# Sixteen rows of a weight load, taken out of the late transfer and fetched early by GpSimd as single packets

## The chip, the cores and the metric

One core of one Trainium2 chip. The metric is the device time of the slowest (here the only) core in microseconds (us), as the median of the timed executions. MB in the profile are 10^6 bytes; a row of 16 KB is 16,384 bytes, a K load of 4096 KB is 4.19 MB.

## The reference

One decoding step: grouped attention over a long cache, a small dense block, and a residual sum. Nearly all the work is reading the two caches from HBM (2 x 134 MB).

```python
# x: (1, 1, 512); k_cache, v_cache: (1, 8, 65536, 128) bf16; 32 query heads, 4 for each K/V head
xn = layernorm(x)
q = xn @ wq                                        # wq: 512 x 4096
p = softmax(q @ k.T * 128 ** -0.5)                 # per head, over 65536 keys
o = p @ v
a = o.reshape(4096) @ wo                           # wo: 4096 x 512, 4.2 MB
b = gelu(xn @ w1 + b1) @ w2 + b2                   # w1: 512 x 1792, w2: 1792 x 512
out = x + a + b
```

## The kernel before

K and V come in sixteen pairs, each of two K loads of 4 MB (slots 0 and 1 of the buffer `kv`) and 8 MB of V (the upper half of `kv`). All big loads are issued by the SP engine into one queue, each as soon as PE has freed its slot. When the last K slots are free, `wo` is loaded into them: three pieces of 2, 1 and 0.5 MB for the first 28 heads, then two pieces for the last four heads.

```python
kv = sb("kv", [128, NSLOT * TPD * DH], BF)          # 4 slots of 32 KB for each partition
...
WP = ...                                            # (0, 4), (4, 2), (6, 1): groups of heads
wo_sb = kv[:, 0:GE * HPG * D].rearrange("p (r n) -> p r n", n=D)
wl_sb = kv[:, wl_at:wl_at + HPG * D].rearrange("p (h n) -> p h n", h=HPG)

def dma_wo():
    for i, (g0, n) in enumerate(WP):
        r = n * HPG
        sch.dma(SP, lambda g0=g0, n=n, r=r: sp.dma_start(
            out=wo_sb[:, g0 * HPG:g0 * HPG + r, :],
            in_=A_wo[g0 * HPG * DH:(g0 + n) * HPG * DH, :].rearrange("(p r) n -> p r n", r=r)),
            wsem[i], writes=[f"wo{i}"] + (["slot0"] if i == 0 else []))
    ...                                             # two wl pieces, into slot 1

for i in range(NU // 2):                            # 16 pairs
    ...
    body(i)                                         # transposes of K, scores, softmax, P @ V
...
for i, (g0, n) in enumerate(WP):                    # the product with wo, at the very end
    for r in range(g0 * HPG, (g0 + n) * HPG):
        for kt in range(KT):
            fin_mm(kt, oX_bf[:, r:r + 1], wo_sb[:, r, kt * 128:(kt + 1) * 128], ["oX", f"wo{i}"], ...)
```

The first piece is the one that the change touches: 128 partitions, 16 KB for each, so 128 rows of 16 KB.

## Time and profile before

| | before |
|---|---|
| time, median of 4 | 658.37 us (658.2 to 658.52) |
| span of the profiled run | 656.5 us |
| bytes moved by the main DMA queue | 280.50 MB |
| PE busy | 82% of the span |
| last landing of a load | 653.7 us |

The page of the kernel before: busy tenths of the DMA engines and GB/s in 40 slices, then the DMA queues (packets, MB, and the time that their packets took, as a share of sixteen engines' span).

```profile
DMA  8999999999999999999999999999999999999997
GB/s 369 438 436 426 429 430 433 439 425 461 401 441 439 421 453 413 437 427 445 433 417 449 417 445 421 427 457 411 447 419 447 429 419 441 423 459 408 431 433 295
...
q1 hardware_dynamic: 8616, 280.50, 99.2%
```

Between the first and the last slice the sixteen DMA engines are busy for 90% or more of every slice. The kernel ends when 280.5 MB have gone through them.

The windows table of the kernel before: for each stretch (us), its length and the busy time of each engine, the granted clock, the DMA share and GB/s.

```profile
240.00:282.00 42.00, 35.85 (x839) 34.23 (x837) 19.97 (x41) 17.32 (x31) 0.09 (x1) 0.80 1.00 432
300.00:600.00 300.00, 254.02 (x6048) 244.33 (x6045) 129.06 (x258) 119.05 (x216) 0.62 (x7) 0.77 1.00 433
634.00:654.00 20.00, 18.06 (x565) 16.43 (x562) 8.09 (x27) 5.14 (x16) 0.09 (x1) 0.68 0.90 376
```

The last but one column is the DMA share: 1.00 in the middle. So I expected time that an engine loses here to move the end (in e2 below it did: 16.6 us lost by the last pair, 16.9 in the time).

The chain that ended last in the kernel before, in order of time (start, length, what): one pair in the middle, and the end.

```profile
237.20 28.38 DMA kv<-in_A_k_cache_dram
265.63 7.16 PE pst L590 x96
275.40 28.96 DMA kv<-in_A_k_cache_dram
...
635.45 1.53 PE pst L590 x24
636.99 16.42 DMA kv<-in_A_wo_dram
```

Of each 38.8 us of a pair the chain spends 28 to 29 in a K load that is on its way, because it was queued behind others: at the 433 GB/s of the table its 4.19 MB alone need 9.7. The last thing that the kernel waits for is `wo`.

Two more facts come from the trace's records of single packets and of semaphore updates. First, the time of a packet follows its bytes: 614 ns for 16 KB, 1216 ns for 32 KB, 2422 ns for 64 KB, 27 GB/s for each engine. Second, every load has sixteen landing marks, as many as it has packets in flight at once (sixteen at 220, 300 and 640 us). I read them as one mark for each DMA engine. Read so, how far apart they lie shows how unequally the engines are loaded:

```
kernel before, landing marks in us     first     9th       last      last - first
a K load                              224.79    225.72    226.80     2.0
a K load one pair later               263.57    264.51    265.58     2.0
a V load                              331.43    332.35    333.42     2.0
last pair, first half of V            632.01    633.12    634.04     2.0
last pair, second half of V           641.73    642.84    643.75     2.0
first wo piece (2 MB)                 646.62    647.74    648.64     2.0
last wo piece                         651.88    652.88    653.73     1.9
```

A difference of 2 us that arose early (0.5 us at 21 us, 2.0 at 72 us) stays to the end, while the DMA share stays near 1.00.

### The profile page before, as it was taken

What the parts mean: (1) busy time and instruction counts of PE and PEld (TensorE: products, weight loads), DVE (VectorE), ACT (ScalarE), POOL (GpSimd) and SP (SyncE); (2) the same over time, 40 slices, a digit from 0 to 9 for tenths busy, and PEclk for the clock granted to TensorE, in tenths of its full rate; (3) what the DMA queues carried; (4) which work ended last, traced back from release to release, by engine and by line L of the source; (5) the groups of instructions that cost most, each with busy time, mean ns of one, the idle gap of its engine ahead of it and who ended that gap; (6) DMA issues with size and microseconds to landing.
All of it is one profiled execution on the core that took longest, in us unless ns stands there. A gap on an engine that the chain in (4) does not pass through costs nothing.

```text
span 656.5 us, 27968 instructions
## 1 busy us (share of the span) xinstructions
PE 539.3 (82%) x12682; PEld 512.1 (78%) x12682; DVE 275.7 (42%) x574; ACT 244.9 (37%) x454; POOL 2.9 (0%) x27
## 2 busy tenths in 40 slices
PE   2388699999789797878969787896978879797897
PEld 0187698988689697868969786896968779686896
DVE  3244162635435172442616245171634516254353
ACT  0134153534425152351605335161443516144251
POOL 0000000000000000000000000000000000000000
PEclk9788597878759596885959778596877859687595
DMA  8999999999999999999999999999999999999997
GB/s 369 438 436 426 429 430 433 439 425 461 401 441 439 421 453 413 437 427 445 433 417 449 417 445 421 427 457 411 447 419 447 429 419 441 423 459 408 431 433 295
DMA packets 8774, 280.65 MB, mean 427 GB/s; under 512 B 1082, under 2 KB 1596, under 8 KB 1724
## 3 DMA queue, kind: packets, MB, share of 16 engines
q1 hardware_dynamic: 8616, 280.50, 99.2%
q8 instruction: 8, 0.13, 0.1%
q10 hardware_dynamic: 148, 0.01, 0.0%
q14 instruction: 2, 0.02, 0.0%
HBM read 280.50 MB, written 0.00 MB: 427 GB/s over the span
## 4 chain that ended last, share of the span: by engine, by line
DMA 63%; PE 34%; issue 2%; DVE 0%; SPq 0%
DMA kv<-in_A_k_cache_dram 61%; PE pst L590 27%; PE pss L610 4%; DMA kv<-in_A_wo_dram 3%; PE pO L681 2%; PE pA L637 0%; PE pA L648 0%; DVE pmax L618 0%; PE pA L697 0%; PE pss L805 0%; DVE gmax L639 0%; DVE diag L641 0%; SPq L470 0%; SPq L467 0%; SPq L463 0%
## 5 line engine op out<-in xcount | busy, mean ns | idle before, releaser
L590 PE MATMUL pst<-ident_bf,kv 128*128 128x128 bf16 x4096 | 284.3, 236 | 34.0 <-DMA kv<-in_A_k_cache_dram 33.9
L600 ACT ACTIVATE kt_ring<-pst 128x1024 bf16<-128x1024 bf16 x192 | 195.6, 1027 | 312.1 <-PE pst L590 310.7
L590 PEld LDWEIGHTS pst<-ident_bf,kv 128*128 128x128 bf16 x4096 | 266.0, 107 | 42.4 <-DMA kv<-in_A_k_cache_dram 35.5
L598 DVE COPY kt_ring<-pst 128x1024 bf16<-128x1024 bf16 x320 | 210.7, 687 | 121.1 <-PE pst L590 118.7
L681 PE MATMUL pO<-P_bf,kv 128*128 128x4 bf16 x4096 | 115.1, 166 | 37.1 <-DMA kv<-in_A_v_cache_dram 32.1
L681 PEld LDWEIGHTS pO<-P_bf,kv 128*128 128x128 bf16 x4096 | 113.6, 104 | 38.5 <-DMA kv<-in_A_v_cache_dram 33.1
L610 PE MATMUL pss<-q_cur,kt_ring 128*128 128x4 bf16 x4096 | 111.9, 164 | 4.9 <-issue 4.9
L610 PEld LDWEIGHTS pss<-q_cur,kt_ring 128*128 128x128 bf16 x4096 | 109.3, 96 | 5.1 <-issue 5.1
L659 ACT ACTIVATE P_bf<-pss,negm 128x128 bf16<-128x128 f32 x128 | 50.9, 547 | 67.6 <-DVE negm L651 67.6
L690 DVE COPY o_all<-pO 128x4 f32 (+1 forms) x32 | 5.2, 161 | 120.3 <-PE pO L681 119.5
L618 DVE TENSOR_REDUCE pmax<-pss 128x4 f32<-128x512 f32 x32 | 22.1, 691 | 68.8 <-PE pss L610 68.8
L659 ACT ACTIVATION_READ_ACCUMULATOR P_bf<-pss,negm 128x1 f32 x128 | 35.3, 276 | 0.0
L648 PEld LDWEIGHTS pA<-diag,ones_f 4*128 4x128 f32 x64 | 12.6, 245 | 17.8 <-DVE diag L641 16.2
L637 PE MATMUL pA<-ident_f,pmax 128*4 128x128 f32 x64 | 14.0, 305 | 12.5 <-DVE pmax L618 12.5
L648 PE MATMUL pA<-diag,ones_f 4*128 4x4 f32 x64 | 15.4, 309 | 10.0 <-DVE diag L641 10.0
L637 PEld LDWEIGHTS pA<-ident_f,pmax 128*4 128x4 f32 x64 | 2.9, 84 | 15.7 <-DVE pmax L618 14.0
L639 DVE TENSOR_REDUCE gmax<-pA 4x1 f32<-4x128 f32 x32 | 8.8, 274 | 9.1 <-PE pA L637 9.1
L673 DVE COPY sums_all<-sums 128x8 f32 (+1 forms) x16 | 2.7, 171 | 23.4 <-ACT P_bf L659 23.4
L697 PE MATMUL pA<-sums_all,ones_f 128*128 128x128 f32 x32 | 12.4, 491 | 0.0
L651 DVE TENSOR_SCALAR negm<-pA 128x4 f32<-128x4 f32 x32 | 5.1, 161 | 10.8 <-PE pA L648 10.8
L697 PEld LDWEIGHTS pA<-sums_all,ones_f 128*128 128x128 f32 x32 | 8.1, 312 | 0.0
L641 DVE TENSOR_SCALAR diag<-ident_f,gmax 4x4 f32<-4x4 f32 x32 | 7.0, 218 | 1.1
(78 smaller groups left out, 49.5 us busy)
## 6 DMA issues: line engine op xcount, KB each, us to landing
kv<-in_A_k_cache_dram SPq DMA_DIRECT2D x32, 4096.0 KB, 27.5
kv<-in_A_v_cache_dram SPq DMA_DIRECT2D x4, 4096.0 KB, 23.2
kv<-in_A_wq_dram SPq DMA_DIRECT2D x1, 4096.0 KB, 12.2
kv<-in_B_w_dram SPq DMA_DIRECT2D x2, 1792.0 KB, 18.0
kv<-in_A_wo_dram SPq DMA_DIRECT2D x1, 2048.0 KB, 23.0
kv<-in_A_wo_dram SPq DMA_DIRECT2D x1, 1024.0 KB, 25.1
kv<-in_A_wo_dram SPq DMA_DIRECT2D x1, 512.0 KB, 25.9
kv<-in_A_wo_dram SPq DMA_DIRECT2D x1, 384.0 KB, 16.4
```

The source lines that it names most:

```text
L590: lambda tb=tb, at=at, b=b, tt=s * TPB + t: pe.transpose(pst[tb][:, at * 128:(at + 1) * 128], slot[b][:, tt, :], ident_bf[:, :]),
L598: e, fn = DVE, lambda tb=tb, dst=dst: dve.tensor_copy(out=dst, in_=pst[tb][:, :])
L600: e, fn = ACT, lambda tb=tb, dst=dst: act.activation(out=dst, in_=pst[tb][:, :], func=ACTF.Copy)
L610: lambda k=k, kb=kb, at=at, t=t: pe.matmul(pss[k][:, at:at + HPG], lhsT=kt_ring[:, kb * BCOL + t * 128:kb * BCOL + (t + 1) * 128], rhs=q_c ...
L618: lambda k=k: dve.tensor_reduce(out=pmax[:, :], in_=pss[k][:, 0:CW].rearrange("p (t j) -> p j t", j=HPG), axis=AX.X, op=ALU.max),
L637: sch.op(PE, lambda: pe.matmul(pA[0:HPG, PA_ST:PA_ST + 128], lhsT=pmax[:, 0:HPG], rhs=ident_f[:, :], start=True, stop=True), reads=["pmax" ...
L639: sch.op(DVE, lambda: dve.tensor_reduce(out=gmax4[:, :], in_=pA[0:HPG, PA_ST:PA_ST + 128], axis=AX.X, op=ALU.max), reads=["pA"], writes=[" ...
L641: sch.op(DVE, lambda: dve.tensor_scalar(out=diag4[:, :], in0=ident_f[0:HPG, 0:HPG], scalar1=gmax4[0:HPG, 0:1], scalar2=None, op0=ALU.mult) ...
L648: sch.op(PE, lambda: pe.matmul(pA[:, PA_SB:PA_SB + HPG], lhsT=ones_f[0:HPG, 0:128], rhs=diag4[0:HPG, 0:HPG], start=True, stop=True), reads ...
L659: lambda k=k, at=at, j=j, src=src: act.activation(out=P_v[k][:, :, j], in_=src[:, :, j], func=ACTF.Exp, bias=negm[:, at:at + 1], scale=1.0 ...
L681: lambda k=k, t=t: pe.matmul(pO[:, 0:HPG], lhsT=vslot[:, k * TPD + t, :], rhs=P_v[k][:, t, :], start=t == 0, stop=t == TPD - 1),
L697: sch.op(PE, lambda: pe.matmul(pA[:, PA_SUM:PA_SUM + NC], lhsT=ones_f[:, :], rhs=sums_all[:, :], start=True, stop=True), reads=["ones_f", ...
```

## The change

The first `wo` piece gets a buffer of its own, `wa`, so it need not wait for slot 0. Of its 128 rows only 112 stay in the late transfer. The other sixteen, partitions 112 to 127, are fetched early, before the fifth pair, by sixteen GpSimd transfers of 8179 elements, one row each. 8179 is a prime number, chosen so that a row is not cut into equal pieces. The 13 elements left of each row come by one small SP transfer. The idea is to have an eighth of the piece out of the way before the end.

```diff
+    NS = 16
+    WA = WP[0][1] * HPG
+    LP = WA * D - 13
+    wa = sb("wa", [128, WA * D], BF)
+    wo_sb = kv[:, WA * D:GE * HPG * D].rearrange("p (r n) -> p r n", n=D)
 ...
+    def dma_rest():
+        for p in range(128 - NS, 128):
+            sch.dma(POOL, lambda p=p: pool.dma_start(out=wa[p:p + 1, 0:LP], in_=src_wa()[p:p + 1, 0:LP]), sem_wa,
+                    writes=["wo0r"], total=16 * NS)
+        sch.dma(SP, lambda: sp.dma_start(out=wa[128 - NS:128, LP:WA * D],
+                                           in_=src_wa()[128 - NS:128, LP:WA * D]), sem_wb, writes=["wo0s"])
+
     def dma_wo():
         for i, (g0, n) in enumerate(WP):
             r = n * HPG
+            if i == 0:
+                sch.dma(SP, lambda: sp.dma_start(out=wa[0:128 - NS, :], in_=src_wa()[0:128 - NS, :]), wsem[i],
+                        writes=["wo0"])
+                continue
 ...
-                wsem[i], writes=[f"wo{i}"] + (["slot0"] if i == 0 else []))
+                wsem[i], writes=[f"wo{i}"] + (["slot0"] if i == 1 else []))
 ...
+        if i == 4:
+            dma_rest()
         body(i)
 ...                                    # and the final product reads wa for the first sixteen heads
```

More of the change, by code (lines that the diff above doesn't have):

```diff
@@ L340, in bass_parallel_sum__gqa_block_cached__dense_activation_gelu__decode_kernel, with wo_row @@
         g0 += n
-    wo_sb = kv[:, 0:GE * HPG * D].rearrange("p (r n) -> p r n", n=D)
+    NS = 16
[3 more added lines that the diff above has]
+    wo_sb = kv[:, WA * D:GE * HPG * D].rearrange("p (r n) -> p r n", n=D)
+    def wo_row(r, cols):
+        return wa[:, r * D + cols.start:r * D + cols.stop] if r < WA else wo_sb[:, r - WA, cols]
     wl_at = TPD * DH
@@ L389, in bass_parallel_sum__gqa_block_cached__dense_activation_gelu__decode_kernel @@
     lsem = [sch.dsem(f"lsem{i}") for i in range(2)]
+    sem_wa, sem_wb = sch.dsem("dwa"), sch.dsem("dwb")
     sem_vb = sch.dsem("dvb")
@@ L473, in bass_parallel_sum__gqa_block_cached__dense_activation_gelu__decode_kernel, with src_wa @@
     WH = (HPG - 1, 1)
+    def src_wa():
+        return A_wo[0:WA * DH, :].rearrange("(p r) n -> p (r n)", r=WA)
+    def dma_rest():
[4 more added lines that the diff above has]
+                                           in_=src_wa()[128 - NS:128, LP:WA * D]), sem_wb, writes=["wo0s"])
     def dma_wo():
@@ L477, in dma_wo @@
             r = n * HPG
+            if i == 0:
+                sch.dma(SP, lambda: sp.dma_start(out=wa[0:128 - NS, :], in_=src_wa()[0:128 - NS, :]), wsem[i],
+                        writes=["wo0"])
+                continue
             sch.dma(SP, lambda g0=g0, n=n, r=r: sp.dma_start(
-                out=wo_sb[:, g0 * HPG:g0 * HPG + r, :],
+                out=wo_sb[:, g0 * HPG - WA:g0 * HPG - WA + r, :],
                 in_=A_wo[g0 * HPG * DH:(g0 + n) * HPG * DH, :].rearrange("(p r) n -> p r n", r=r)),
-                wsem[i], writes=[f"wo{i}"] + (["slot0"] if i == 0 else []))
+                wsem[i], writes=[f"wo{i}"] + (["slot0"] if i == 1 else []))
         h0 = 0
@@ L812, in bass_parallel_sum__gqa_block_cached__dense_activation_gelu__decode_kernel @@
             for kt in range(KT):
-                fin_mm(kt, oX_bf[:, r:r + 1], wo_sb[:, r, kt * 128:(kt + 1) * 128], ["oX", f"wo{i}"], False, False,
+                fin_mm(kt, oX_bf[:, r:r + 1], wo_row(r, slice(kt * 128, (kt + 1) * 128)), ["oX", f"wo{i}"] + ["wo0r", "wo0s"] * (i == 0), False, False,
                        r == (g0 + n) * HPG - 1 and kt == KT - 1)
```

## The prediction

> **What bounds it now.** The DMA engines, nearly from end to end. The page's queue part has the main queue busy 99.2% of the span (280.5 MB, 427 GB/s); the windows table has a DMA share of 1.00 at 433 GB/s for 200 to 600 us. The trace's packets of 16, 32 and 64 KB take 614, 1216 and 2422 ns: time follows bytes, 27 GB/s per engine. The SP queue issues each K load 27.5 us (median) before it lands, of which 4 MB needs 9.7: large slack. PE is 82% busy but waits for K and V. The chain of waits ends in 16.4 us of "DMA kv<-wo"; the last landing is at 653.7, the span ends at 656.5.
>
> The sixteen landing marks of each transfer differ by 2.0 us from about 70 us to the end: five engines are 1.7 to 2 us behind the foremost, after instruction fetches (16 KB, 1.02 to 1.12 us each, 27 to 84 us). The span ends with the last of them.
>
> **What the change does.**
> - It removes no bytes. 112 rows of 16 KB stay in the last loads (7 per engine, not 8: 0.61 us less there); 16 rows move to about 217 us, when the fifth V has landed.
> - The first wo piece loses its wait for slot 0 (12.7 us on the SP queue). It ends at 625.6, when two V halves (8 MB, landing 634.0 and 643.7) are still queued, so no engine starved for it. Gain about 0.
> - The 13 elements left over: 16 descriptors of 26 bytes. The trace's 28-byte packets take 9 ns. Under 0.1 us.
> - GpSimd: 16 issues, in the 38.8 us between two V flags.
> - PE, DVE, ACT: the same order of instructions.
>
> **How the early rows share the engines.** [...]sixteen transfers give one row to each engine. No run here shows it yet. Then every engine carries as many bytes as before: +0.61 us early, -0.61 us late. Against it: all sixteen rows lie in partitions 112 to 127[...]. I expect a loss of 0 to 2 us.
>
> **Predicted:** 658.9 us, range 657.0 to 661.3. Faster by over 2%: 0.01; within 2%: 0.97; slower by over 2%: 0.02.
>
> **What would show it.** Right: a new GpSimd queue with 16 packets of 16 KB near 217 to 245 us; K and V landings after 260 us are 0.5 to 2 us later than before; the last wo landing still closes the chain; the first wo piece is issued near 613 but lands only after V, near 648. The spread of the landing marks stays 2 us or grows to 3.
>
> **What would make it wrong.** If [...]all 16 rows fall on one engine, it carries 15 more rows: 15 x 0.61 = 9 us later (667). If the engines that get or lose rows happen to be the laggards, the spread shrinks and up to 1.5 us is won. If an issue takes several us, a V flag is late. If packets of a second queue cost double, as the instruction fetches do, 0.5 us more is lost.

The forecast's sum: 658.4 us before, 0.61 us more for each engine early and 0.61 less late (a row of 16 KB took 614 ns), under 0.1 us for the leftover, and a loss of 0 to 2 us for the early rows; it came to 658.9 us. Three passages are cut. They argued why the rows would spread over the engines, and why rows on sixteen neighbouring partitions would cost something, which gave the 0 to 2 us. No trace or run of this case shows the rules that they rested on. So "one row to each engine" and the 0 to 2 us stand as assumptions. In the expectations of the experiments, the clauses that rested on such rules are cut too.

## The result, and the profile after

| | before | after |
|---|---|---|
| time, median of 4 | 658.37 us | 679.06 us (678.16 to 679.52) |
| span of the profiled run | 656.5 us | 677.6 us |
| MB of all packets | 280.65 | 280.65 |

The change is slower by 20.7 us, far above the predicted range (657.0 to 661.3). The ratio is 1.0313 (95% interval 1.0295 to 1.0331). Ratios here are the mean time of one kernel's fast runs over that of the other's of the same rounds, so they are not quite the ratio of the medians quoted.

The page of the kernel after: the same parts as shown of before.

```profile
DMA  9999999999999999997999999999999999999993
GB/s 371 433 459 403 430 433 449 433 418 449 418 449 418 438 412 402 436 408 308 433 431 429 433 433 427 431 422 433 433 414 453 414 445 416 449 427 420 431 304 119
...
q1 hardware_dynamic: 8632, 280.24, 97.5%
q0 software_dynamic: 512, 0.26, 0.2%
```

The bytes are the same. A new queue, q0, holds the GpSimd transfers: 512 packets for 16 transfers, of which 16 carry a row (16,358 bytes) and 496 are of 4 bytes. Slice 19 (from 305 us) falls to 308 GB/s with a busy digit of 7, and the last slice (from 661 us) to 119 with a 3: there some engines have nothing to do. The slice before the last (from 644 us) moves only 304 GB/s although its digit is 9: there the engines are busy, and their packets take longer (the 16 KB packets of the 112 rows 1088 ns on average instead of 614).

The windows table after:

```profile
240.00:282.00 42.00, 23.29 (x598) 22.11 (x596) 10.32 (x23) 9.18 (x23) 0.09 (x1) 0.67 0.98 408
300.00:600.00 300.00, 248.31 (x5963) 238.59 (x5960) 122.67 (x251) 113.76 (x211) 0.70 (x8) 0.76 0.99 424
650.00:675.00 25.00, 18.96 (x570) 16.52 (x567) 8.37 (x28) 5.43 (x18) 0.09 (x1) 0.65 0.64 179
```

Between 240 and 282 us PE works 23.3 us instead of 35.9: it waits. The chain after says for what:

```profile
239.09 40.99 DMA kv<-in_A_k_cache_dram
280.13 7.97 PE pst L613 x96
290.72 29.05 DMA kv<-in_A_k_cache_dram
...
651.74 1.53 PE pst L613 x24
653.28 20.87 DMA kv<-in_A_wo_dram
```

One K load is in the chain for 41.0 us instead of 28.4, and the wo load at the end for 20.9 instead of 16.4. These are two separate steps. GpSimd issued its sixteen transfers just before the first of them, in one go (the timeline of GpSimd after: start, length, what):

```profile
217.17 0.09 POOL L456 MEMSET flag<- 1x1 f32 x1 [38.73 <-DMA kv<-in_A_v_cache_dram]
217.72 8.30 POOL L489 DMA_DIRECT2D wa<-in_A_wo_dram  x16 [0.46 <-issue]
266.23 0.09 POOL L456 MEMSET flag<- 1x1 f32 x1 [40.21 <-DMA kv<-in_A_v_cache_dram]
```

An issue took 0.52 us, and the flag of the sixth V was late only because the V was. GpSimd itself is not in the way.

The landing marks answer most of the question:

```
kernel after, landing marks in us      first    15th     last     last of before   later by
a K load                              224.77   227.26   228.08    226.80            1.3
a K load one pair later               264.15   268.46   280.09    265.58           14.5
a V load                              339.09   339.62   348.84    333.42           15.4
a K load                              543.99   545.84   553.38    537.03           16.4
last pair, first half of V            641.16   643.06   650.37    634.04           16.3
last pair, second half of V           650.91   654.60   665.17    643.75           21.4
first wo piece (1.75 MB)              658.75   662.32   669.41    648.64           20.8
last wo piece                         665.49   667.19   674.47    653.73           20.7
```

From the second line on a single engine is late, 7 to 12 us behind the fifteenth. The loss comes in three terms. The early step is 15.4 us (up to the V load). A slow growth of 0.9 us follows, up to the last pair. The late step is 4.4 us (20.7 - 16.3), at the time when the 112 rows are loaded.

The packet records show the late step on the late engine itself, which can be followed there, since it alone still moves V after 653.7 us. It has V left to load when the other engines begin the 112 rows (their packets run from 650.4 to 661.4 us). Five of its V packets of 32 KB, from 651.25 us on, take 2373, 2328, 2262, 2352 and 1746 ns instead of 1216: 5.0 us too much. Its own seven rows come after that, when the others are done with the piece, and take 611 to 618 ns each. They are one fewer than before, which gives 0.6 us back.

The single packets show the early step at work. This is from the packet records of the kernel after; each line begins within 20 ns of where the one before ends:

```
start us   took ns   queue      bytes
226.179     1525     q1         32768
227.700      774     q0         16358    a row
228.461     1538     q1         32768
231.215      782     q0         16358    a row   (after one more packet of q1)
```

The sixteen rows follow each other like this, between 221.9 and 280.1 us, and never overlap. They take turns with packets of the main queue, one or two of these between two rows. A row takes 755 ns on average and the 32 KB packet after it about 320 ns more than its 1216. So a row costs this engine about 1.08 us, not the 0.61 of 16 KB in the main queue.

My theory then (A): all sixteen rows go through one engine, and the 112-row transfer is slow by itself. The rivals: (B) the rows are spread over the engines and hinder each other, since all are written to sixteen neighbouring partitions; (C) the second queue or GpSimd costs something in itself; and for the late step, that it only follows from the late engine.

### The profile page after: what moved, and what is told of

Read it like the earlier page. It is cut to its first block, busy times and chain, and to the rows that moved or that the text cites. A ratio compares the mean times of both kernels' runs of the same rounds, so it can differ in the third digit from the quotient of the medians.

```text
span 677.6 us, 27986 instructions
## 1 busy us (share of the span) xinstructions
PE 539.3 (80%) x12682; PEld 511.3 (75%) x12682; DVE 275.7 (41%) x574; ACT 245.2 (36%) x454; POOL 11.2 (2%) x43
## 2 busy tenths in 40 slices
DMA packets 9303, 280.65 MB, mean 414 GB/s; under 512 B 1611, under 2 KB 2125, under 8 KB 2253
## 4 chain that ended last, share of the span: by engine, by line
DMA 64%; PE 33%; issue 2%; DVE 0%; SPq 0%
DMA kv<-in_A_k_cache_dram 61%; PE pst L613 26%; PE pss L633 4%; DMA kv<-in_A_wo_dram 3%; PE pO L704 2%; PE pA L660 0%; PE pA L671 0%; DVE pmax L641 0%; PE pA L720 0%; PE pss L830 0%; DVE gmax L662 0%; DVE diag L664 0%; SPq L479 0%; SPq L476 0%; SPq L472 0%
## 5 line engine op out<-in xcount | busy, mean ns | idle before, releaser
L671 PE MATMUL pA<-diag,ones_f 4*128 4x4 f32 x64 | 15.4, 309 | 10.0 <-DVE diag L664 10.0
L456 POOL MEMSET flag<- 1x1 f32 x16 | 1.4, 88 | 652.8 <-DMA kv<-in_A_v_cache_dram 614.1
L489 POOL DMA_DIRECT2D wa<-in_A_wo_dram x16 | 8.3, 527 | 0.5 <-issue 0.5
## 6 DMA issues: line engine op xcount, KB each, us to landing
kv<-in_A_wo_dram SPq DMA_DIRECT2D x1, 384.0 KB, 20.9
```

Source lines behind the costliest of these rows:

```text
L489: sch.dma(POOL, lambda p=p: pool.dma_start(out=wa[p:p + 1, 0:LP], in_=src_wa()[p:p + 1, 0:LP]), sem_wa, writes=["wo0r"], total=16 * NS)
L671: sch.op(PE, lambda: pe.matmul(pA[:, PA_SB:PA_SB + HPG], lhsT=ones_f[0:HPG, 0:128], rhs=diag4[0:HPG, 0:HPG], start=True, stop=True), reads ...
```

## The experiments

Eleven kernels ran, all with correct results. Variants called "late load of all 128" fetch all 128 rows of the piece again at the end, after waiting for the early ones. The early rows are then redundant, and the early step stands alone. The common part of those is:

```diff
-                sch.dma(SP, lambda: sp.dma_start(out=wa[0:128 - NS, :], in_=src_wa()[0:128 - NS, :]), wsem[i],
-                        writes=["wo0"])
+                sch.dma(SP, lambda: sp.dma_start(out=wa[:, :], in_=src_wa()), wsem[i],
+                        writes=["wo0", "wo0r", "wo0s"])
```

| run | early rows | late load | time us | before, same chip | ratio |
|---|---|---|---|---|---|
| e1 | none | 128 rows | 658.40 | 658.39 | 1.0000 |
| e2 | 16 single GpSimd rows, 112-127 | 128 rows | 675.25 | 658.39 | 1.0260 |
| e3 | one SP transfer of rows 112-127 | 112 rows | 666.74 | 658.39 | 1.0122 |
| e4 | 16 GpSimd rows of 8192 elements | 128 rows | 662.45 | 658.39 | 1.0059 |
| e5 | 4 GpSimd transfers of 4 rows | 128 rows | 667.88 | 658.44 | 1.0139 |
| e6 | 8 single rows, 112-119 | 128 rows | 665.25 | 658.44 | 1.0106 |
| e7 | 8 single rows, 0-3 and 32-35 | 128 rows | 661.59 | 658.44 | 1.0049 |
| e8 | 16 single rows, issued by SP | 128 rows | 677.19 | 658.44 | 1.0288 |
| e9 | none | 64 + 64 rows | 664.94 | 658.49 | 1.0102 |
| e10 | 16 single rows, 0-15 | 128 rows | 672.57 | 658.49 | 1.0215 |
| e11 | first 1024 columns of all 128 rows | the other 7168 columns | 658.49 | 658.49 | 0.9999 |

### e1: the buffer alone

The late load of all 128, and no `dma_rest()`.

> The control: the new buffer alone, all 128 rows in one late SP transfer, nothing from GpSimd. Every theory that puts the loss into the sixteen early rows or into the 112-row load expects the time of before, 658.4 us within 0.5, and landing marks of the wo pieces as before (last at 653.7). If the time is above 660, the buffer or the earlier place in the queue costs something itself.

Measured: 658.40 us, ratio 1.0000 (0.9983 to 1.0016). The buffer and the missing wait for slot 0 neither cost nor win anything. The prediction was right in this.

### e2: the early rows alone

The late load of all 128, `dma_rest()` as in the change.

> The sixteen GpSimd rows as in the change, but the late load takes all 128 rows again (the sixteen are loaded twice, with the same bytes, the second time after waiting for the first). Theory A (one engine carries all sixteen rows, about 1.08 us each, and the 112-row load is a second, separate cost): 658.4 + 15.5 + 0.8 at the early step, no step of 5 us at the V1/wo stage, so 674 to 676 us, with one engine 9 us or more behind the others. Theory B (the rows are spread over the engines[...]): no single laggard. If the late step of 5 us is only a consequence of the laggard and not of 112 rows: 679 to 680 us.

Measured: 675.25 us, 16.9 above before. One engine is over 6 us behind the fifteenth to the end. The last pair's first half of V lands 16.6 us later than before and the last wo piece 16.6 us later: there is no late step. So the early rows cost 16.6 us by themselves, the slow growth included. The step of 4.4 us belongs to the 112-row load, and does not follow from the late engine, which is here too.

### e3: the sixteen rows in one transfer

```diff
-        for p in range(128 - NS, 128):
-            sch.dma(POOL, ...)
-        sch.dma(SP, ...)
+        sch.dma(SP, lambda: sp.dma_start(out=wa[128 - NS:128, :], in_=src_wa()[128 - NS:128, :]), sem_wb,
+                writes=["wo0r", "wo0s"])
```

> The sixteen rows by one SP transfer of 16 rows at the same place, the late load with 112 rows as in the change. Theory A: one row for each engine, so no laggard; the early step falls below 2 us and the late load of 112 rows still costs 3 to 5 us: 661 to 664 us. Theory B[...]: [...]the early step stays and the time is 674 us or more. If the 112-row load costs nothing without the laggard: 658.5 to 660 us.

Measured: 666.74 us, a miss for both theories. Theory A is right that the step of 15 us is gone: no single engine is far behind. But in the profiled run (668.62 us, the slowest of four) the early transfer still costs 4.6 us (the K load of 226.80 before lands at 231.44) instead of under 2, and the late step is 5.6 us. In the packet records the packets of the main queue beside the early transfer take half as long again to twice their time: of the sixteen packets in flight at 217.0 us, one for each engine, eight are of 32 KB with 1.9 to 2.5 us (usual: 1.2) and eight of 64 KB with 3.8 to 5.1 (usual: 2.4). The 16 KB packets of the late load take 1103 ns on average, against 614 before. This fits the hindrance that B named; how it comes about was not shown. It is not what made the change's early step of 15.4 us, but not a small thing either: sixteen rows of 16 KB, 0.6 us of bytes if each engine carries one, cost 4.6 us this way.

### e4: whole rows, a length that 16 divides

```diff
-    LP = WA * D - 13
+    LP = WA * D
```

The small SP transfer is left out with it; late load of all 128.

> GpSimd transfers of whole rows (8192 elements, divisible by 16) in place of 8179, no leftover; the late load takes all 128 rows again. Theory A1 (one engine because 8179 is prime[...]): now each row is cut into sixteen pieces, all engines share, 658.8 to 661 us, and the GpSimd queue has 256 packets of 1 KB. Theory A2 (one partition means one engine, whatever the length): 16 packets of 16 KB on one engine, 674 to 676 us.

Measured: 662.45 us. The q0 queue now has 256 packets of 1 KB in place of sixteen of 16 KB, so each row is cut into sixteen pieces, and the single late engine is gone (last and fifteenth mark are 0.2 us apart at the end). So it was the length, 8179 instead of 8192, that put each row on one engine. The time is 1.5 us above the range: the last engine loses 4.2 us where the range left room for 0.4 to 2.6. The reason was not shown.

### e5: does the first engine move on?

```diff
-        for p in range(128 - NS, 128):
-            sch.dma(POOL, lambda p=p: pool.dma_start(out=wa[p:p + 1, 0:LP], ...
+        for a, n in [(112, 4), (116, 4), (120, 4), (124, 4)]:
+            sch.dma(POOL, lambda a=a, n=n: pool.dma_start(out=wa[a:a + n, 0:LP], in_=src_wa()[a:a + n, 0:LP]), sem_wa,
+                    writes=["wo0r"], total=16 * 4)
```

> Four GpSimd transfers of four rows (4 x 8179 elements[...]) in place of sixteen of one row; late load of all 128 rows. If the first engine of each transfer moves on by the number of engines used[...], the sixteen rows fall on sixteen engines: no engine over 3 us behind after 300 us, 660 to 663 us. If every transfer starts at the same engine[...], four engines carry four rows each: they end 3 to 5 us behind the rest (4 x 1.08, less up to 2 us of lead): 662 to 665 us, and the landing marks after 300 us show a group of four late ones.

Measured: 667.88 us, outside both ranges. The landing marks alone don't decide, since all engines are late: the first mark of the V load of 333 us comes 5.5 us later than before, the last 9.7. The packet records decide. The nine packets below follow each other end to start within 10 ns each time, so they are read as one engine's, and four rows are among them:

```
start us   took ns   queue      start us   took ns   queue
221.92      1076     q0 row     230.29       949     q0 row
222.99      2684     q1         231.24      2168     q1
225.68      1213     q1         233.41      1215     q1
226.88       939     q0 row     234.62      1026     q0 row
227.83      2462     q1
```

So one engine carried one row of each of the four transfers: the first engine did not move on. The same records show how all engines lost. Of the sixteen packets in flight at 223.95 us, one is a row (1.88 us) and the other fifteen are 32 KB packets that take 2.0 to 3.5 us instead of 1.2; the same happens twice more (1.9 to 3.3 us at 228.2, 1.9 to 3.4 at 231.3). Each of these transfers writes four neighbouring partitions. Why the packets of the other engines take longer meanwhile was not shown.

### e6 and e7: eight rows, on two kinds of partitions

```diff
-        for p in range(128 - NS, 128):
+        for a, n in [(p, 1) for p in range(112, 120)]:                      # e6
+        for a, n in [(p, 1) for p in (0, 1, 2, 3, 32, 33, 34, 35)]:         # e7
```

> Half the single rows: eight GpSimd transfers, rows 112 to 119; late load of all 128. One engine at 1.08 us for each row, which led by about 2 us: 8 x 1.08 - 2 = 6.6 us behind, so 665 to 667 us. If the loss is a fixed cost of having such transfers and not of the rows, it stays near 675.

> Eight single rows again, but those of partitions 0 to 3 and 32 to 35[...]. [...]the packets take 0.61 and the time is 661 to 663 us (8 x 0.61 - 2 = 2.9). If the extra cost is that of the second queue, it is 665 to 667 us as with rows 112 to 119.[...]

The first range of e7 is for a cost that depends on which partitions a row is written to.

Measured: 665.25 us (6.8 above before) and 661.59 us (3.15 above). The rows take 756 ns in e6, and the packets after them 325 ns too long. In e7 a row takes 611 ns, and the packet after it is not longer at all (2 ns less on average). Both agree with the sums written before: 8 x 1.08 - 2.0 = 6.6 and 8 x 0.61 - 2.0 = 2.9, where 2.0 is the lead that this engine had. So the second queue costs nothing by itself here. The two runs differ only in the partitions that the rows are written to (756 ns on 112 to 119, 611 ns on 0 to 3 and 32 to 35). So the partitions make a row dear or cheap; by what mechanism was not shown.

### e8: the same single rows from SP

```diff
-            sch.dma(POOL, lambda p=p: pool.dma_start(...
+            sch.dma(SP, lambda p=p: sp.dma_start(...
```

> The sixteen single-row transfers of 8179 elements issued by SP in place of GpSimd, in the main queue; late load of all 128. They all go to one engine here too. Packets in the same queue without alternation: if each costs 0.61 us, 16 x 0.61 - 2 = 7.8 us, 666 to 668 us; if 0.75 to 0.8 us[...], 668 to 671 us; if 1.08 us as on GpSimd, 674 to 676 us.

Measured: 677.19 us, above all three ranges, though again one engine is far behind (over 14 us behind the fifteenth in the next K load). In the main queue the rows stand behind each other without packets between them, from 214.5 to 233.5 us, so one row takes 1.19 us, about twice 0.61. 16 x 1.19 - 2.0 = 17 us. The K load of 226.80 before lands at 244.00, 17.2 us later; the rest of the loss of 18.8 comes afterwards and was not tested. That GpSimd issued the rows is not the reason.

### e9: the late load in two halves

```diff
-                sch.dma(SP, lambda: sp.dma_start(out=wa[0:128 - NS, :], in_=src_wa()[0:128 - NS, :]), wsem[i],
-                        writes=["wo0"])
+                for h in range(2):
+                    sch.dma(SP, lambda h=h: sp.dma_start(out=wa[64 * h:64 * h + 64, :], in_=src_wa()[64 * h:64 * h + 64, :]),
+                            wsem[i], writes=["wo0"], total=32)
```

No `dma_rest()`.

> Nothing early, nothing from GpSimd; the late load of 128 rows cut into two SP transfers of 64 rows (partitions 0 to 63, then 64 to 127). Each engine still moves eight rows of 16 KB. [...]its 16 KB packets take about 1.2 us instead of 0.61 and the late load takes up to 4.9 us longer: 661 to 664 us. If the 112-row load is slow for another reason (its odd shares of seven rows)[...], the time is that of before, 658.4 within 0.6.

The first range is for a transfer to fewer than 128 partitions that is slow for that alone.

Measured: 664.94 us, 6.45 above before, 0.9 above the range. The last landing marks agree with before within 0.25 us from 200 us up to the last pair's first half of V (634.21 against 634.04); after that, the second wo piece is 6.7 us later. The 16 KB packets take 1111 ns on average. Nothing was loaded early here, and no share is odd: 128 rows over sixteen engines are eight for each, if they are shared evenly as before. It is enough that each transfer covers 64 partitions instead of 128 (1111 ns instead of 614).

```
mean time of the 16 KB packets of the late load, ns
before 614   e1 614   e2 615        128 rows in one transfer
after 1088   e3 1103                112 rows
e9 1111                             64 and 64 rows
```

### e10: single rows of partitions 0 to 15

As e2, with rows 0 to 15 in place of 112 to 127.

> Sixteen single GpSimd rows again, but partitions 0 to 15 in place of 112 to 127; late load of all 128. [...]the first four data packets take 611 ns and the next twelve about 750 ns, in this order, and the time is about 1.5 to 2 us below the 675.25 of the early rows alone: 672 to 674.5 us. [...]all sixteen take 611 ns and the time is about 666 us.

The first range is for rows 0 to 3 as cheap as in e7 and the others dear, the second for sixteen cheap rows.

Measured: 672.57 us, 2.7 below e2. The sixteen rows took, in order of issue: 612, 611, 611, 611, then 673, 781, 791, 768, 701, 769, 813, 774, 695, 799, 791 and 771 ns. The first four are cheap and all others dear, just as written before. So here too the cost of a row goes with its partition: 611 to 612 ns on 0 to 3, 673 to 813 on 4 to 15.

### e11: columns instead of rows

```diff
-        for p in range(128 - NS, 128):
-            sch.dma(POOL, ...)
-        sch.dma(SP, ...)
+        sch.dma(POOL, lambda: pool.dma_start(out=wa[:, 0:1024], in_=src_wa()[:, 0:1024]), sem_wa,
+                writes=["wo0r", "wo0s"])
 ...
-                sch.dma(SP, lambda: sp.dma_start(out=wa[0:128 - NS, :], in_=src_wa()[0:128 - NS, :]), wsem[i],
+                sch.dma(SP, lambda: sp.dma_start(out=wa[:, 1024:], in_=src_wa()[:, 1024:]), wsem[i],
```

> The repaired form: the same 256 KB early on the GpSimd queue, but as the first 1024 columns of all 128 partitions in one transfer, and the other 7168 columns of all 128 partitions late. [...]If the loss came from one engine[...], nothing is left of it: 658.0 to 659.2 us, all landing marks within 0.8 us of before from 300 us on. If the second queue or GpSimd itself costs something, more than 660 us.

Measured: 658.49 us, ratio 0.9999 (0.9983 to 1.0016). The DMA queues of e11:

```profile
q1 hardware_dynamic: 8616, 280.24, 99.1%
q0 software_dynamic: 80, 0.26, 0.1%
```

The same 0.26 MB go through the same GpSimd queue at nearly the same moment (the transfer lands by 228.5 us), and the whole loss is gone. The landing marks stay about 1 us later than before, which is over the 0.8 that I had allowed, but 0.4 us of that were there before the early transfer (217.51 against 217.09 in a V load), and at the end they are 0.5 us later. There is no gain either: the bytes are the same and the engines were never idle. No experiment points to a version that beats both kernels, so none was made.

## Why the prediction was wrong

- **The bound: right.** DMA engines, from end to end. e11 shows that moving an eighth of the piece earlier wins nothing as long as the engines are full.
- **The own buffer and the lost wait for slot 0: right**, gain 0 (e1). The first wo piece was issued 12 us before slot 0 was free (629.3, the next at 641.9), and landed behind V all the same.
- **GpSimd issue time and the V flags: right.** 8.3 us for sixteen issues; the flags were not late by it.
- **"Sixteen transfers give one row to each engine": wrong, and this is the step that failed.** All sixteen went to one engine. e2 shows the early rows to cost 16.9 us alone; e4, which only makes the length divisible by 16, takes away all but 4 of them; e5 shows one engine carry a row of each of four transfers of four rows. The length does what the change meant it to do: 8179 elements came as one packet of 16,358 bytes, 8192 as sixteen of 1 KB. That each next transfer would begin at another engine, which the prediction needed, was an assumption, and it does not fit these transfers. Why they all began at the same engine was not shown.
- **The price of that branch, 0.61 us per row: too small.** The prediction named this branch and priced it at 9 us. Measured: 0.755 us for the row and 0.32 us for the packet behind it, 1.08 us. 16 x 1.08 - 2.0 of lead = 15.3 us, against an early step of 15.4. The prediction had seen a packet of another queue cost nearly double (the instruction fetches, 1.02 to 1.12 us for 16 KB), and gave it 0.5 us. e7 shows that the price hangs on the partitions: on 0 to 3 and 32 to 35 a row costs 0.61 and nothing after it.
- **"-0.61 late": right for the late engine's own rows, wrong as the late step,** which was 4.4 us longer. The late engine did have one row fewer (0.6 us less). But while the other engines loaded the 112 rows, at 1088 ns for a packet on average instead of 614, its V packets took 5.0 us too long. In e2, with one engine late too and 128 rows loaded by the others, V packets took at most 1226 ns at this stage, and there is no late step. The prediction asked what the partitions of the sixteen rows that left would cost, and not those of the 112 that stayed. e3 has a late step of 5.6 us from the 112 rows without a late engine, and e9 shows a like effect for 64 and 64 rows with nothing else changed. Why 112 rows are slow stays open: no run loads them with nothing early.
- **The loss of "0 to 2 us" by the early rows: too small,** had the rows been spread. In e3 no single engine is far behind, and they cost 4.6 us. e3 shows longer packets beside the early rows, but not why.
- **The spread of landing marks, "2 or 3 us": wrong;** it is 9 to 17 us, by one engine.

The sum: 15.4 (one engine) + 0.9 (growth) + 4.4 (112 rows, through the late engine's V packets) = 20.7 us. The growth of 0.9 us between 333 and 634 us was not tested. In that stretch the engines that are ahead wait for slots and start new V loads together, and several V packets of 64 KB take up to 4 us instead of 2.4 at such moments. That could be enough, but it is argued, not shown.

## What to carry to other kernels

When the DMA engines are the bound, count bytes for each engine and not for the whole: one engine with sixteen extra rows of 16 KB set the time of a kernel that moves 280 MB (16.6 us in e2). The 16 KB packets of the late load took 614 ns when it covered all 128 partitions, and about 1100 when it covered 112 or 64; to split such a load, cut columns and not partitions (e11 cost 0 us, cutting rows 3 to 21). The spread of the sixteen landing marks of a transfer shows such an imbalance at a glance, in the first transfer after it begins (here a K load with its first mark at 264.15 us and its last at 280.09).
